# The up products of a gated MLP: copied out of PSUM by ScalarE and multiplied in SBUF, instead of multiplied out of PSUM by VectorE

## The chip, the core and the metric

The kernel runs on one core of a Trainium2 chip. The metric is the device time of one execution in microseconds (us), as the median of several runs. Engines are named as in the profile: PE (TensorE; PEld is its weight load), ACT (ScalarE), DVE (VectorE), POOL (GpSimd), SP (SyncE, which issues the DMAs here).

## What is computed

```python
xn = _layernorm(x)                                   # x: 2048 x 512, bfloat16
return x + _A_ref(xn, wqkv, w_phi, wo) + _B_ref(xn, w_gate, w_up, w_down)

# A: linear attention, 32 heads of 16
pq = einsum("bhsd,hdf->bhsf", q, w_phi); pk = einsum("bhsd,hdf->bhsf", k, w_phi)
phi_q = concat([softmax(pq), softmax(-pq)]);  phi_k = concat([softmax(pk), softmax(-pk)])
kv = einsum("bhsf,bhsd->bhfd", phi_k, v);  z = sum of phi_k over s
o = (phi_q @ kv) / (phi_q @ z + 1e-6);  A = o @ wo

# B: gated MLP, hidden width 1792
g = xn @ w_gate;  u = xn @ w_up;  B = (g * u) @ w_down
```

The change touches `g * u` alone.

## The kernel before, in words

Tokens come in 16 tiles of 128 (index t) and in 4 groups of 512 (index g). All inputs are loaded once by DMAs that SP issues at the start; everything then lives in SBUF. PSUM has 8 banks of 128 x 512 fp32.

- `emit_ln_stats` and `emit_xn` (lines 403 to 433): DVE takes mean and variance (L406, L408, L412), POOL the power -0.5 (L414), DVE normalises (L428), PE transposes the tile by four 128x128 matmuls, ACT copies the result out of PSUM into `xnT`.
- `k_pe` (L494): the V product of a tile, 4 matmuls of 128x512, copied out by ACT.
- `k_pk` and `q_pk` (L499, L575): the K and Q products with the feature map folded into the weights (`wprime`, L438), 4 matmuls each. Then `emit_exp` (L451): ACT copies the product twice, plain and negated, into SBUF; DVE takes a maximum tree (L464, four steps) and subtracts it (L470); ACT takes the exponential of 128x1024.
- `k_norm`, `q_scale` (L504, L580): sums (L484), reciprocals and scalings on DVE.
- `emit_kv` (L540): the K-V products, 8 matmuls of 128x65 per head group and half.
- `q_T`, `q_num`, `q_oT` (L592 to L611): a DMA transposes the weights of a tile, PE takes 8 small matmuls of 128x68, DVE divides (L602, L603), another DMA transposes the result into `oT`.
- `glu` (L520): 56 pieces, 4 token groups by 14 blocks of 128 hidden units. A piece is two products of 4 matmuls of 128x512, gate into bank `bg` and up into bank `bu`. ACT copies the gate bank to a bfloat16 tile `gr` in a ring of three (L531); DVE multiplies the up bank by `gr` into `hT` (L533). The pieces turn through banks 5, 6 and 7; those of the last token group through 5 and 6.
- `final` (L616): the output of a tile, 14 matmuls over `hT` and 4 over `oT` into one bank; DVE adds x (L635), and a DMA stores the tile.

ACT operations all carry the line of the helper `act_op`, L273; all matmuls have L292; DMAs have L162 (transposes) and L163.

What sets the order: all these steps are recorded first. `_order` (L696) then lists them engine by engine, with a planned cost for each: it takes whatever step can start first, and among those of an engine that are equally early the one of least priority number. Copies out of a product bank of `glu` and the multiplication have priority -1, ahead of everything else that is ready. The matmuls of `glu` have priorities of 1e6 and more and those of `final` of 2e6 and more, so PE takes them when nothing else is ready. The order that results is fixed in the program: each engine runs its list strictly in turn, and `_emit_all` (L752) puts semaphore waits where a step depends on another engine. A changed cost or a changed dependence thus changes the lists of every engine.

Of the kernel before, what the change touches and what calls it, by code (L numbers as in the profile page):

```python
# [8 lines left out]
ALU = mybir.AluOpType  # L9
# [184 lines left out]
def _build(nc, es, A_x, A_wqkv, A_w_phi, A_wo, B_w_gate, B_w_up, B_w_down, out):  # L194
# [59 lines left out]
    def sbv(name, lo, n):  # L254
        off = layout[name] + lo
        return arena[:, off:off + n]
# [5 lines left out]
    def bank(b, lo=0, n=512):  # L262
        return psum[:, b * 512 + lo: b * 512 + lo + n]
# [4 lines left out]
    def act_op(out_ap, in_ap, func=ACTF.Copy, scale=1.0, bias=None, prio=None):  # L268
        def fn(e):
            kw = {}  # L270
            if bias is not None:
                kw["bias"] = bias
            return e.activation(out=out_ap, in_=in_ap, func=func, scale=scale, **kw)  # L273
        r = [in_ap]
        if isinstance(scale, bass.AP):
            r.append(scale)
        if isinstance(bias, bass.AP):
            r.append(bias)
        return sc.step(ACT, fn, reads=r, writes=[out_ap], cost=50.0 + 0.833 * in_ap.free_size(), lat=180.0, prio=prio)

    def dve(fn, reads, writes, n, rate=1.0, fixed=65.0, prio=None):
        return sc.step(DVE, fn, reads=reads, writes=writes, cost=fixed + rate * n / 0.96, lat=150.0, prio=prio)
# [4 lines left out]
    def mms(items, prio=None, warm=False):  # L287

        def fn(e):
            ins = None  # L290
            for o, l, r, a, z in items:
                ins = e.matmul(o, lhsT=l, rhs=r, start=a, stop=z)  # L292
            return ins
        reads = []
        writes = []
        c = 0.0
        for o, l, r, a, z in items:
            reads += [l, r]
            writes.append(o)
            c += max(25.0, o.free_size() / 2.4 + 2.3) * (1.6 if warm else 1.0)  # L300
        return sc.step(PE, fn, reads=reads, writes=writes, cost=c, lat=260.0, prio=prio)

    def group(o, pairs):
        n = len(pairs)
        return [(o, l, r, i == 0, i == n - 1) for i, (l, r) in enumerate(pairs)]
# [13 lines left out]
    def xnT(q, s_lo, n):  # L319
        return sbv("xnT", q * S_TOK + s_lo, n)  # L320
# [62 lines left out]
    for jt in range(NQ):  # L383
        pool(lambda e, jt=jt: e.tensor_tensor(
            out=wbd_v[:, jt, :].rearrange("p (g f b) -> p g f b", g=2, b=4),
            in0=wphi_v[:, jt, None, :, None].to_broadcast([128, 2, 16, 4]),
            in1=bind8.rearrange("p (g b) -> p g b", g=2)[:, :, None, :].to_broadcast([128, 2, 16, 4]), op=ALU.mult),
# [127 lines left out]
    def hT(g, ft, lo, n):  # L515
        return sbv("hTa" if g < 2 else "hTb", ((g % 2) * NF + ft) * 512 + lo, n)
# [3 lines left out]
    def glu(g, ft, banks):  # L520
        i = glu_ctr[0]
        glu_ctr[0] += 1
        bg = banks[(2 * i) % len(banks)]
        bu = banks[(2 * i + 1) % len(banks)]
        gr = sbv("gring", (i % 3) * 512, 512)
        base = 1e6 + i * 10
        mms(group(bank(bg), [(wg_v[:, q, ft * 128:(ft + 1) * 128], xnT(q, g * 512, 512)) for q in range(NQ)]),
            prio=base)
        mms(group(bank(bu), [(wu_v[:, q, ft * 128:(ft + 1) * 128], xnT(q, g * 512, 512)) for q in range(NQ)]),
            prio=base + 1)  # L530
        act_op(gr, bank(bg), prio=-1.0)  # L531
        dst = hT(g, ft, 0, 512)
        dve(lambda e: e.tensor_tensor(out=dst, in0=bank(bu), in1=gr, op=ALU.mult), [bank(bu), gr], [dst], 512,  # L533
            prio=-1.0)


# [106 lines left out]
    def some_glu(n, g_max):  # L643
        for _ in range(n):
            if units and units[0][0] <= g_max:
                glu(*units.pop(0), (5, 6, 7) if units and units[0][0] < 3 else (5, 6))
# [189 lines left out]
```

## Time and profile before

| | |
|---|---|
| median of 3 runs | 229.64 us (229.61 to 229.78) |
| profiled execution | 230.12 us, of which the span of the profile is 228.0 us |
| clock granted to PE | 1.00 in every slice |
| ACT 128x512 out of PSUM | 160 of 608 ns (L273) |
| ACT 128x1024 exponential | 32 of 1061 ns (L273) |
| DVE 128x512 product out of PSUM | 56 of 681 ns (L533) |
| DVE waiting for ACT at L464 | 2.0 us in all |
| ACT waiting for DVE at L470 | 28.1 us in all, 14 times |
| ACT waiting for PE | 45.7 us in all, 48 times |

The engines' busy times are unions of the rows' durations. Two instructions that follow each other on ACT or DVE overlap in these rows: six copies of 128x512 that ACT makes one after another take 3.04 us, so one starts about 0.48 us after the other although each row lasts 0.6 us. The same holds for DVE (a row of 0.68 us, the next one 0.60 us later).

### The profile page before, as it was taken

The numbers are of one execution on the slowest core, as the hardware profiler recorded it, in microseconds if no ns is written. First come the engines' busy times: TensorE is split into PE (matmuls) and PEld (weight loads), VectorE is DVE, ScalarE is ACT, GpSimd is POOL, SyncE is SP. The second block draws the span as 40 slices with busy tenths as digits, with TensorE's granted clock in tenths as the row PEclk, the third lists the DMA queues.
The fourth block names the chain that finished last, engine by engine and source line by source line (L and its number), as shares of the span: only waits on it lengthen the run. The fifth ranks groups of instructions, "written<-read, shape, count | busy, mean of one in ns | idle before, by whom it ended". The sixth has DMA issues, their size and how long they took to land.

```text
span 228.0 us, 3617 instructions
## 1 busy us (share of the span) xinstructions
PE 219.0 (96%) x1306; PEld 108.9 (48%) x1330; DVE 193.7 (85%) x554; ACT 119.7 (52%) x201; POOL 8.2 (4%) x22
## 2 busy tenths in 40 slices
PE   8899799999999999999999999999999999998994
PEld 8454354444454555444464444444445444444441
DVE  4548999999997999999986999999999999993321
ACT  2587997735449987944528585464653331110000
POOL 5301000000011000000000000000000000000000
PEclk9999999999999999999999999999999999999999
DMA  6999970000000000000000035554144545468301
GB/s 181 249 285 369 379 249 1 0 0 0 0 3 1 0 3 0 0 3 0 0 4 0 0 65 96 85 94 103 36 92 105 118 92 116 92 126 110 88 23 46
DMA packets 39697, 18.33 MB, mean 80 GB/s; under 512 B 30720, under 2 KB 38656, under 8 KB 39680
## 3 DMA queue, kind: packets, MB, share of 16 engines
q1 hardware_dynamic: 39152, 18.09, 32.5%
q8 instruction: 10, 0.16, 0.3%
q10 hardware_dynamic: 528, 0.02, 0.1%
q14 instruction: 7, 0.06, 0.1%
HBM read 8.67 MB, written 2.10 MB: 47 GB/s over the span
## 4 chain that ended last, share of the span: by engine, by line
PE 85%; SPq 6%; DMA 5%; DVE 1%; issue 1%; ACT 1%
PE ps L292 85%; SPq L162 4%; DMA arena<-in_A_x_dram 3%; DMA arena<-arena 2%; SPq L163 1%; ACT arena L273 1%; DVE arena L464 1%; DVE arena L406 0%; DVE arena L635 0%; DVE arena L470 0%
## 5 line engine op out<-in xcount | busy, mean ns | idle before, releaser
L292 PE MATMUL ps<-arena 128*128 128x512 bf16 (+3 forms) x1306 | 219.0, 328 | 6.1 <-ACT arena L273 2.4
L292 PEld LDWEIGHTS ps<-arena 128*128 128x128 bf16 x1330 | 108.9, 100 | 115.7 <-DVE arena L533 2.3
L273 ACT ACTIVATE arena<-ps 128x512 bf16<-128x512 f32 (+1 forms) x168 | 88.0, 590 | 50.6 <-PE ps L292 45.7
L484 DVE TENSOR_TENSOR arena<-arena 128x512 f32<-128x512 bf16 (+3 forms) x128 | 49.3, 395 | 0.2
L273 ACT ACTIVATE arena<-arena 128x1024 bf16<-128x1024 bf16 x32 | 34.0, 1061 | 29.0 <-DVE arena L470 28.1
L533 DVE TENSOR_TENSOR arena<-ps,arena 128x512 bf16<-128x512 f32 x56 | 38.1, 681 | 2.2 <-PE ps L292 1.6
L464 DVE TENSOR_TENSOR arena<-arena 128x128 bf16<-128x128 bf16 (+3 forms) x128 | 31.7, 269 | 2.2 <-ACT arena L273 2.0
L470 DVE TENSOR_TENSOR arena<-arena 128x1024 bf16<-128x1024 bf16 x32 | 21.6, 676 | 0.0
L635 DVE TENSOR_TENSOR arena<-ps,arena 128x512 bf16<-128x512 f32 x16 | 11.0, 688 | 11.8 <-PE ps L292 11.5
L406 DVE BATCH_NORM_STATS2 arena<-arena 128x6 f32<-128x512 bf16 x16 | 10.5, 682 | 6.8 <-DMA arena<-in_A_x_dram 6.8
L603 DVE TENSOR_TENSOR arena<-ps,arena 128x512 bf16<-128x512 f32 x16 | 10.9, 680 | 0.1
L511 DVE TENSOR_TENSOR arena<-arena 128x1024 bf16<-128x1024 bf16 x16 | 10.9, 680 | 0.0
L602 DVE RECIPROCAL arena<-ps 128x32 f32<-128x32 f32 x16 | 5.6, 350 | 4.6 <-PE ps L292 4.3
L508 DVE RECIPROCAL arena<-arena 128x64 bf16<-128x64 f32 x16 | 8.7, 543 | 0.1
L428 DVE TENSOR_SCALAR arena<-arena 128x512 bf16<-128x512 bf16 x16 | 5.9, 409 | 2.2 <-POOL arena L414 2.0
L414 POOL TENSOR_TENSOR arena<-arena 128x1 f32<-128x1 f32 (+1 forms) x7 | 5.2, 750 | 60.7 <-DVE arena L412 60.7
L589 DVE TENSOR_TENSOR arena<-arena 128x512 bf16<-128x512 bf16 x16 | 6.6, 414 | 0.0
L586 DVE RECIPROCAL arena<-arena 128x32 f32<-128x32 f32 x16 | 5.5, 342 | 0.0
L587 DVE TENSOR_TENSOR arena<-arena 128x32 bf16<-128x32 f32 x16 | 2.7, 171 | 0.0
L273 ACT ACT_TABLE_LOAD x1 | 1.3, 1283 | 1.3 <-PEq L821 1.3
L408 DVE BATCH_NORM_AGGREGATE arena<-arena 128x2 f32<-128x6 f32 x16 | 1.9, 162 | 0.0
L551 DVE TENSOR_TENSOR arena<-arena 128x64 bf16<-128x64 f32 x8 | 1.7, 214 | 0.0
(18 smaller groups left out, 8.4 us busy)
## 6 DMA issues: line engine op xcount, KB each, us to landing
out_dram<-arena SPq DMA_DIRECT2D x16, 128.0 KB, 1.7
arena<-in_B_w_down_dram SPq DMA_DIRECT2D x1, 1792.0 KB, 15.4
arena<-in_B_w_gate_dram SPq DMA_DIRECT2D x1, 1280.0 KB, 9.1
arena<-in_B_w_up_dram SPq DMA_DIRECT2D x1, 1280.0 KB, 11.9
arena<-in_A_x_dram SPq DMA_DIRECT2D x1, 1024.0 KB, 6.5
arena<-in_A_x_dram SPq DMA_DIRECT2D x2, 256.0 KB, 3.2
arena<-in_A_wqkv_dram SPq DMA_DIRECT2D x1, 512.0 KB, 5.2
arena<-in_B_w_gate_dram SPq DMA_DIRECT2D x1, 512.0 KB, 4.4
```

What stands on the lines that cost most here:

```text
L162: return e.dma_start_transpose(out_ap, in_ap)
L273: return e.activation(out=out_ap, in_=in_ap, func=func, scale=scale, **kw)
L292: ins = e.matmul(o, lhsT=l, rhs=r, start=a, stop=z)
L406: dve(lambda e, t=t: e.bn_stats(stats_v[:, t, 0:6], x_tile(t)), [x_tile(t)], [stats_v[:, t, 0:6]], 512)
L464: dve(lambda e, dst=dst, src=src, k=k: e.tensor_tensor(out=dst, in0=src[:, :, 0:k], in1=src[:, :, k:2 * k], op=ALU.max), [src], [dst], 16 ...
L470: dve(lambda e: e.tensor_tensor(out=p4, in0=p4, in1=src[:, :, None, :].to_broadcast([128, 16, 16, 4]), op=ALU.subtract), [pst, src], [pst] ...
L484: dve(lambda e, dst=dst, src=src, k=k: e.tensor_tensor(out=dst, in0=src[:, :, 0:k], in1=src[:, :, k:2 * k], op=ALU.add), [src[:, :, 0:2 * ...
L508: dve(lambda e: e.reciprocal(out=rs, in_=sm), [sm], [rs], 64, rate=8.0)
L511: dve(lambda e: e.tensor_tensor(out=e4, in0=e4, in1=r4[:, :, None, :].to_broadcast([128, 16, 16, 4]), op=ALU.mult), [ek_v[:, t, :], rs], [ ...
L533: dve(lambda e: e.tensor_tensor(out=dst, in0=bank(bu), in1=gr, op=ALU.mult), [bank(bu), gr], [dst], 512, prio=-1.0)
L603: dve(lambda e: e.tensor_tensor(out=o.rearrange("p (g h d) -> p g h d", g=8, h=4), in0=nd[:, :, 0:64].rearrange("p g (h d) -> p g h d", h= ...
L635: dve(lambda e: e.tensor_tensor(out=og, in0=bank(b), in1=x_tile(t), op=ALU.add), [bank(b), x_tile(t)], [og], 512, prio=-2.0)
```

## The change

```diff
         act_op(gr, bank(bg), prio=-1.0)
         dst = hT(g, ft, 0, 512)
-        dve(lambda e: e.tensor_tensor(out=dst, in0=bank(bu), in1=gr, op=ALU.mult), [bank(bu), gr], [dst], 512,
+        act_op(dst, bank(bu), prio=-1.0)
+        dve(lambda e: e.tensor_tensor(out=dst, in0=dst, in1=gr, op=ALU.mult), [dst, gr], [dst], 512, rate=0.5,
             prio=-1.0)
```

Each of the 56 pieces gets a second ACT copy, which puts the up product as bfloat16 where the result will stand. DVE then multiplies that tile in place by the gate tile, both bfloat16 in SBUF. The planned cost of the multiplication is halved (`rate=0.5`). An up bank is free again when ACT has copied it, no longer when DVE has multiplied it. Since the costs and the dependences differ, `_order` also makes another order; how many instructions each engine runs is otherwise the same.

## The prediction

> **What bounds the kernel now.** The page's busy times name PE:
>
> ```profile
> PE 219.0 (96%) x1306; PEld 108.9 (48%) x1330; DVE 193.7 (85%) x554; ACT 119.7 (52%) x201; POOL 8.2 (4%) x22
> ```
>
> PE's waits, from the view of who waited for whom (total us, times, longest), come to under 5 us:
>
> ```profile
> PE ps L292 <- ACT arena L273: 2.4, 3, 1.6
> PE ps L292 <- DVE arena L363: 1.1, 1, 1.1
> PE ps L292 <- DMA arena<-arena: 0.8, 1, 0.8
> PE ps L292 <- DVE arena L428: 0.5, 2, 0.3
> ```
>
> And two pieces of the chain that ended last (start, length, what, matmuls):
>
> ```profile
> 118.20 10.74 PE ps L292 x49
> ...
> 217.81 7.30 PE ps L292 x33
> ```
>
> A busy PE need not be a full PE, since matmul rows overlap (379 ns each). The chain settles it: 49 recorded matmuls of 128x512 in 10.74 us are one per 219 ns, and start to start the trace shows 216 ns with one record lost in each such piece. So PE runs at its own rate from 24.89 us to its end at 225.1 us (217.81 + 7.30), but for one gap of 0.81 us before 208.01. The other waits lie before 24.9 us, the largest being 1.64 us. The change takes no matmul away, so **the floor does not move**: it can win at most the two gaps, 1.64 + 0.81 = 2.45 us, and it can lose as much as ACT holds PE up.
>
> **The two gaps.** The timeline of the first (start, length, engine, instruction, idle before):
>
> ```profile
> 22.49 0.68 DVE L470 TENSOR_TENSOR arena<-arena 128x1024 bf16<-128x1024 bf16 x1
> ...
> 23.20 1.06 ACT L273 ACTIVATE arena<-arena 128x1024 bf16<-128x1024 bf16 x1 [2.10 <-DVE arena L470]
> 23.87 0.68 DVE L533 TENSOR_TENSOR arena<-ps,arena 128x512 bf16<-128x512 f32 x1
> 24.17 1.06 ACT L273 ACTIVATE arena<-ps 128x512 bf16<-128x512 f32 x2
> 24.47 0.68 DVE L470 TENSOR_TENSOR arena<-arena 128x1024 bf16<-128x1024 bf16 x1
> ...
> 24.89 0.60 PE L292 MATMUL ps<-arena 128*128 128x128 bf16 x5 [1.64 <-ACT arena L273]
> ```
>
> PE stops at 23.09 (its last matmul starts at 22.875) because the transposition of token tile 7 needs a bank that ACT empties at 24.17, and in ACT's list that copy stands behind the exponential of 23.20, which needed DVE's subtraction of 22.49. The second gap:
>
> ```profile
> 207.44 1.24 SPq L162 DMA_TRANSPOSE arena<-arena  x1
> ...
> 208.01 1.29 PE L292 MATMUL ps<-arena 128*128 128x68 bf16 x11 [0.81 <-DMA arena<-arena]
> ```
>
> A transposed weight tile (t = 14) landed at 207.97 while PE had nothing ahead of it in its list but that. Its first parts had landed at 206.08; a 16 KB packet of the queue q8, which fetches instructions, ran from 205.62 for 1.39 us on one of the DMA engines.
>
> **The change part by part.** Durations are those of the groups kept apart by shape:
>
> ```profile
> L273 ACT ACTIVATE arena<-ps 128x512 bf16<-128x512 f32 x160 | 86.9, 608 | 50.6 <-PE ps L292 45.7 <-DVE arena L484 4.3
> L533 DVE TENSOR_TENSOR arena<-ps,arena 128x512 bf16<-128x512 f32 x56 | 38.1, 681 | 2.2 <-PE ps L292 1.6 <-ACT arena L273 0.2
> L273 ACT ACTIVATE arena<-arena 128x1024 bf16<-128x1024 bf16 x32 | 34.0, 1061 | 29.0 <-DVE arena L470 28.1 <-DMA arena<-arena 0.9
> ...
> L464 DVE TENSOR_TENSOR arena<-arena 128x512 bf16<-128x512 bf16 x32 | 13.3, 416 | 2.0 <-ACT arena L273 2.0
> ```
>
> *VectorE.* 56 rows of 681 ns become 56 of the bfloat16 form in SBUF, whose nearest row is the first step of the maximum tree, 416 ns at the same shape: 38.1 - 56 x 0.416 = 38.1 - 23.3 = 14.8 us less work, 193.7 to about 179 us. None of it is on PE's path where PE is full: worth 0 there.
>
> *ScalarE.* 56 more copies of 608 ns: 34.0 us, 119.7 to about 154 us (67%). At the spacing of 0.48 us that copies in a row show (six in 3.04 us) it is 27 us. One piece asks PE for 8 x 0.216 = 1.73 us and ACT for 0.96 instead of 0.48 us. In the K stage a tile costs PE 4 + 4 matmuls and a transposition, 1.95 us, and ACT four copies and an exponential at 0.96 us, 2.9 us; the 28 pieces of the first two token groups, spread over the last 12 tiles (2.33 a tile), make this PE 5.98 against ACT 5.14 us, 86%, where it was 4.0 us, 67%. So on the average of every stage **ACT stays under PE**, with a thin margin in the K stage. Taking the order into account, two stretches of 6 us are full already (columns: PE, PEld, DVE, ACT, POOL):
>
> ```profile
> 30.00:36.00 6.00, 5.95 (x35) 2.94 (x34) 6.00 (x15) 6.00 (x12) 0.00 (x0) 1.00 0.48 150
> ...
> 72.00:78.00 6.00, 5.95 (x34) 2.99 (x34) 5.74 (x18) 5.96 (x11) 0.00 (x0) 1.00 0.00 0
> ```
>
> *The first gap, by the new lists.* Up to the second matmul group of piece 1 PE's list is unchanged, so PE is free at 23.09 as before. Then it has piece 2 and piece 3 (16 matmuls, not 4) ahead of the transposition of tile 7. Up 2 and gate 3 find their banks emptied (copies at about 20.5 and 21.4) and fill 2 x 0.864 us, to 24.82. Up 3 needs gate 2's copy. ACT's list has it behind the exponentials of tiles 0 and 1. The first still starts at 23.20. The second's subtraction no longer stands behind a multiplication of 0.60 us on DVE: it ends at 24.55 instead of 25.15; exponential 24.58 to 25.54, copy to 26.15. PE loses 26.2 - 24.82 = 1.38 instead of 1.80 us (24.89 - 23.09): 0.42 better. But ACT then has nine copies and an exponential queued, and the next tiles' products need the copies of tiles 6 and 7, which it reaches at 30.3 and 31.3: 0.17 and 0.07 late, and about 0.05 for one bank before: 0.3 worse. I take **-0.1 us**. Bounds: -1.64 (no gap left) and +0.96 (one exponential more ahead of a needed copy). No load is late: piece 4, which moves up from 35.6 to about 28.2 us, needs weights that landed at 23.8 and 27.2; 1 us of cover.
>
> *The second gap.* DVE and ACT get through the Q stage earlier against PE: after the last group of 128x68 PE has 137 matmuls left instead of 65, 29.6 us. The last transposed tiles are then no longer needed at once. **-0.8 us**; bounds -0.81 and 0. SP's list keeps its order of transposes and stores and issues nothing more. But the q8 fetches come about every 20 us whatever the order (ten in the trace, at 143.1 and 163.1 among them), and a transposed tile in flight then lands up to 1.4 us late; the tiles of t = 5 and 9 come close to those two, with 0.6 us and more of room: **+0.1 us** (0 to 0.8). [...]
>
> *New waits in the middle.* Both banks of a piece now wait for one engine. Where ACT stands at an exponential whose subtraction is not done (14 times, 28.1 us, in the row ACT <- DVE L470), two copies a piece stand behind it instead of one, and DVE can no longer empty the up bank. With banks 5 to 7 PE runs one and a half pieces, 2.6 us, ahead. Most of those waits are harmless because the list puts an exponential only where ACT had nothing else. I take **+0.3 us**; bounds 0 and +1.9 (four copies of 0.48 us in the two full stretches, all pushed on to PE).
>
> *Sum.* -0.1 - 0.8 + 0.1 + 0.3 = -0.5 us: 230.12 to 229.6 us in the profiled execution. The median, 0.48 us under that execution, goes to **229.1 us**. What lies after PE's last matmul (0.69 us of DVE and the last store) is unchanged.
>
> **Rivals.**
> 1. *The gap only moves.* Another transposed tile is hit, or the second gap is partly the profiled execution's own (it is the slower one by 0.48 us); the rest as above. 229.64 - 0.1 + 0.3 = 229.8, between 229.3 and 230.0. For it: q8's fetches stay. Against it: 14 of the 16 tiles were in time before.
> 2. *ACT becomes the bound in the K stage* (other side). The place is the stretches 30 to 36 and 72 to 78 us, where ACT has no idle time; it decides once ACT is asked for more than PE's time over a stretch longer than the 2.6 us that the banks cover. Four copies more there cost 1.9 us; with the second gap gone: 229.64 + 1.9 - 0.8 = 230.7, 231.5 with it. For it: 86% on average leaves little for uneven work. Against it: PE's list was made anew with the new costs. [...]
> 3. *Both gaps close*: 229.64 - 1.64 - 0.81 + 0.3 = 227.5. It needs exponential 0 earlier than 23.20, and what precedes it (x landing at 20.55, DVE's queue) is untouched.
>
> That the multiplication keeps its 681 ns is possible, but then PE is full all the same and the time is that of rival 1.
>
> **How the numbers follow.** A measurement of this kernel can tell about 0.2% (0.46 us) from no change, so faster means under 229.18. Forecast (228.6 to 229.5): 0.48, of it 0.31 faster and 0.17 same. Rival 1: 0.22, same but for 0.03 faster. Rival 2: 0.22, slower but for 0.02 same. Rival 3: 0.08, faster. Together faster 0.42, same 0.38, slower 0.20. The range takes in the forecast, rival 1 and the lower half of each of the others: 228.2 to 230.7.
>
> **What would show it.** L534 near 416 ns; ACT 154 us; PE <- ACT still with a wait near 25 us, of 1.4 instead of 1.6 us; no PE <- DMA after 200 us. Wrong: PE <- ACT or PEld <- ACT with many waits between 30 and 130 us (rival 2), PE <- DMA earlier (rival 1), a first wait well under 1 us (rival 3).

## The result, and the profile after

The changed kernel takes **230.37 us** (median, 230.24 to 230.68), the kernel before in the same rounds 229.63 us: ratio 1.0033, 95% interval 1.0022 to 1.0043. It is 0.74 us slower. The forecast was 229.1 us (228.2 to 230.7). The profiled execution took 230.26 us with a span of 228.3 us (before 230.12 and 228.0), PE at a granted clock of 1.00. In some executions of four of the kernels below the granted clock was 0.992 or 0.993 instead of 0.998 to 1.000, and these took 231.6 to 232.9 us; without them the median of the kernel with the change in the Q stage alone is 230.14 instead of 230.29 us, and that of the kernel with x loaded earlier 230.28 instead of 231.01 us.

Busy times of the engines:

```profile
PE 218.8 (96%) x1306; PEld 107.1 (47%) x1330; DVE 180.9 (79%) x554; ACT 145.7 (64%) x257; POOL 8.4 (4%) x22
```

Groups, forms kept apart (busy us, mean ns | idle before, and whom it waited for):

```profile
L273 ACT ACTIVATE arena<-ps 128x512 bf16<-128x512 f32 x216 | 116.3, 633 | 29.2 <-PE ps L292 27.9 <-DVE arena L484 0.4
L273 ACT ACTIVATE arena<-arena 128x1024 bf16<-128x1024 bf16 x32 | 34.9, 1089 | 9.3 <-DVE arena L470 9.2
L534 DVE TENSOR_TENSOR arena<-arena 128x512 bf16<-128x512 bf16 x56 | 23.5, 420 | 2.7 <-ACT arena L273 2.6
```

The operations cost what the prediction said: the multiplication 420 ns, 12.8 us less on DVE, 26.0 us more on ACT, which is 56 times 0.46 us. ACT's wait for subtractions fell from 28.1 to 9.2 us: it no longer stands idle, it has work. Whom PE waits for (total us, times, longest):

```profile
PE ps L292 <- ACT arena L273: 2.0, 4, 1.0
PE ps L292 <- DVE arena L428: 1.3, 1, 1.3
PE ps L292 <- DVE arena L363: 1.1, 1, 1.1
PE ps L292 <- DMA arena<-arena: 1.0, 1, 1.0
```

PE's own timeline from 20 us on (start, length, instruction, matmuls; in brackets the idle time before, where the rows show one):

```profile
25.82 47.24 PE L292 MATMUL ps<-arena 128*128 128x512 bf16 x247 [1.00 <-ACT arena L273]
73.31 66.29 PE L292 MATMUL ps<-arena 128*128 128x512 bf16 x438 [0.24 <-ACT arena L273]
140.60 84.82 PE L292 MATMUL ps<-arena 128*128 128x68 bf16 x465 [1.00 <-DMA arena<-arena]
```

The reader is to see three things. The gap near 25 us is there, smaller. The gap of 208 us is gone, and one of 1.00 us stands before 140.60 instead. And there is a break at 73.31 where before had none. A row of a matmul lasts longer than its turn (379 against 216 ns), so waits under about 0.15 us hide in these lines. Taken start to start (216 ns for a 128x512; records missing from the trace taken out), between 36 and 110 us PE stands 0.67 us: 0.10 at 46.24, 0.05 at 71.17, 0.19 at 73.09, 0.15 at 89.21, all for a bank that ACT has yet to empty (the first matmul after the third wait is missing from the trace, so its row begins at 73.31), and 0.18 at 107.74 for DVE's copy of the K-V products. Before, the same count finds nothing between 36 and 207 us.

The start, with the gap that the prediction worked out:

```profile
22.62 1.06 ACT L273 ACTIVATE arena<-arena 128x1024 bf16<-128x1024 bf16 x1 [0.84 <-DVE arena L470]
...
24.00 1.06 ACT L273 ACTIVATE arena<-arena 128x1024 bf16<-128x1024 bf16 x1 [0.32 <-DVE arena L470]
...
24.96 2.04 ACT L273 ACTIVATE arena<-ps 128x512 bf16<-128x512 f32 x4
...
25.82 6.42 PE L292 MATMUL ps<-arena 128*128 128x512 bf16 x30 [1.00 <-ACT arena L273]
```

Two exponentials, then the copy of gate 2, and PE goes on: the order that was foretold. All of it lies earlier than foretold because the second half of x (tiles 8 to 15), whose statistics stand in DVE's list ahead of the first subtraction, landed at 19.97 us, in the execution of before at 20.55. That is 0.58 us of chance between the two profiles, and so they differ by only 0.3 us in their spans while the medians differ by 0.74.

The new gap, in the chain that ended last, and SP beside it:

```profile
135.78 4.78 DMA arena<-arena
140.55 0.05 issue
140.60 5.18 PE ps L292 x30
```

The transposed tile t = 4 took 4.78 us from its issue to its landing (the median of the 32 transposes of this trace is 3.0 us). Its parts landed from 138.79 to 140.55; a 16 KB packet of q8, a fetch of instructions, ran from 138.34 for 1.28 us. (The page gives the kind `instruction` to q8, with 10 packets and 0.16 MB, and to q14, with 7 and 0.06 MB.) In before the fetch of 205.62 stood so beside t = 14.

What ACT does to PE, by stretches (PE, PEld, DVE, ACT and POOL busy us, clock, DMA share, GB/s), first before, then after:

```profile
36.00:48.00 12.00, 11.95 (x56) 5.42 (x56) 11.95 (x30) 8.19 (x15) 0.00 (x0) 1.00 0.00 0
...
sum 72.00, PE 71.63 PEld 34.66 DVE 69.49 ACT 48.53 POOL 2.02; mean PE 11.94 PEld 5.78 DVE 11.58 ACT 8.09 POOL 0.34
```

```profile
36.00:48.00 12.00, 11.95 (x56) 5.32 (x56) 11.71 (x41) 11.76 (x22) 0.00 (x0) 1.00 0.00 0
...
sum 72.00, PE 71.37 PEld 34.88 DVE 66.92 ACT 63.40 POOL 2.13; mean PE 11.89 PEld 5.81 DVE 11.15 ACT 10.57 POOL 0.35
```

Between 36 and 108 us ACT went from 48.5 to 63.4 of 72 us, 88%. It is not the bound on the average, but it is nearly full, and its list is strictly in turn. At one of the breaks:

```profile
71.38 1.16 ACT L273 ACTIVATE arena<-arena 128x1024 bf16<-128x1024 bf16 x1
...
72.32 2.66 ACT L273 ACTIVATE arena<-ps 128x512 bf16<-128x512 f32 x5
...
73.08 1.41 PEld L292 LDWEIGHTS ps<-arena 128*128 128x128 bf16 x8 [0.51 <-ACT arena L273]
...
73.31 1.46 PE L292 MATMUL ps<-arena 128*128 128x512 bf16 x6 [0.24 <-ACT arena L273]
```

The second copy of the row of five empties the bank; it stands behind an exponential and another copy, with no idle time on ACT in between.

### The profile page after: what moved, and what is told of

Read it like the earlier page. It is cut to its first block, busy times and chain, and to the rows that moved or that the text cites. A ratio compares the mean times of both kernels' runs of the same rounds, so it can differ in the third digit from the quotient of the medians.

```text
span 228.3 us, 3639 instructions
## 1 busy us (share of the span) xinstructions
PE 218.8 (96%) x1306; PEld 107.1 (47%) x1330; DVE 180.9 (79%) x554; ACT 145.7 (64%) x257; POOL 8.4 (4%) x22
## 4 chain that ended last, share of the span: by engine, by line
PE 81%; SPq 6%; DMA 5%; DVE 4%; ACT 3%; issue 1%
PE ps L292 81%; SPq L162 4%; ACT arena L273 3%; DMA arena<-in_A_x_dram 3%; DMA arena<-arena 2%; SPq L163 1%; DVE arena L464 1%; DVE arena L470 1%; DVE arena L484 0%; DVE arena L406 0%; DVE arena L636 0%; DVE arena L604 0%; DVE arena L603 0%; DVE arena L534 0%; DVE arena L587 0%
## 5 line engine op out<-in xcount | busy, mean ns | idle before, releaser
L292 PEld LDWEIGHTS ps<-arena 128*128 128x128 bf16 x1330 | 107.1, 99 | 117.9 <-ACT arena L273 7.2
L273 ACT ACTIVATE arena<-ps 128x512 bf16<-128x512 f32 (+1 forms) x224 | 117.2, 619 | 29.2 <-PE ps L292 27.9
L484 DVE TENSOR_TENSOR arena<-arena 128x128 f32<-128x128 f32 (+3 forms) x128 | 49.4, 396 | 1.1 <-ACT arena L273 0.8
L273 ACT ACTIVATE arena<-arena 128x1024 bf16<-128x1024 bf16 x32 | 34.9, 1089 | 9.3 <-DVE arena L470 9.2
L464 DVE TENSOR_TENSOR arena<-arena 128x256 bf16<-128x256 bf16 (+3 forms) x128 | 31.2, 272 | 2.0 <-ACT arena L273 1.8
L636 DVE TENSOR_TENSOR arena<-ps,arena 128x512 bf16<-128x512 f32 x16 | 11.1, 691 | 26.0 <-PE ps L292 25.8
L534 DVE TENSOR_TENSOR arena<-arena 128x512 bf16<-128x512 bf16 x56 | 23.5, 420 | 2.7 <-ACT arena L273 2.6
L604 DVE TENSOR_TENSOR arena<-ps,arena 128x512 bf16<-128x512 f32 x16 | 10.9, 679 | 0.1
L428 DVE TENSOR_SCALAR arena<-arena 128x512 bf16<-128x512 bf16 x16 | 6.0, 409 | 2.6 <-POOL arena L414 2.3
L590 DVE TENSOR_TENSOR arena<-arena 128x512 bf16<-128x512 bf16 x16 | 6.5, 403 | 0.0
```

What stands on the lines that cost most here:

```text
L464: dve(lambda e, dst=dst, src=src, k=k: e.tensor_tensor(out=dst, in0=src[:, :, 0:k], in1=src[:, :, k:2 * k], op=ALU.max), [src], [dst], 16 ...
L484: dve(lambda e, dst=dst, src=src, k=k: e.tensor_tensor(out=dst, in0=src[:, :, 0:k], in1=src[:, :, k:2 * k], op=ALU.add), [src[:, :, 0:2 * ...
L534: dve(lambda e: e.tensor_tensor(out=dst, in0=dst, in1=gr, op=ALU.mult), [dst, gr], [dst], 512, rate=0.5, prio=-1.0)
L604: dve(lambda e: e.tensor_tensor(out=o.rearrange("p (g h d) -> p g h d", g=8, h=4), in0=nd[:, :, 0:64].rearrange("p g (h d) -> p g h d", h= ...
L636: dve(lambda e: e.tensor_tensor(out=og, in0=bank(b), in1=x_tile(t), op=ALU.add), [bank(b), x_tile(t)], [og], 512, prio=-2.0)
```

## The experiments

Theory A: a fetch of instructions that falls on a transposed tile makes that tile late, and which tile it falls on follows from how many instructions PE has issued, not from the clock. Theory F: the gap near 25 us is there because DVE's list stands at the statistics of tiles whose load has not landed. Theory G: the waits between 36 and 110 us come from ACT's work a tile, since ACT alone now empties the banks of a piece. Other theories are told in the expectations. "Before" is each time the kernel before, timed beside the run.

### The fetches moved, by the warm-up alone

The 50 matmuls that warm PE up at the start become fewer and longer, or more and shorter, with the same columns in all. Only the number of PE's instructions ahead of the work changes.

```diff
-    warm = sbv("tree", 0, 128)
-    mms([(bank(7, 0, 128), warm, warm, True, True)] * 50, warm=True)
+    warm = sbv("tree", 0, 256)
+    mms([(bank(7, 0, 160), warm[:, 0:128], warm[:, 0:160], True, True)] * 40, warm=True)   # changed form
+    mms([(bank(7, 0, 104), warm[:, 0:128], warm[:, 0:104], True, True)] * 62, warm=True)   # before form
```

> The changed kernel, but PE's 50 warm-up matmuls of 128x128 at the start are 40 of 128x160: 20 PE rows fewer for the same columns, so each instruction fetch on q8 should come about 1.6 us later against PE's work, and the lists of all engines are otherwise the same. Theory A (the 1.16 us gap at 139 us is a fetch that delays one transposed tile, t = 4): the fetch comes at about 140 us, after that tile has landed, the gap goes, no wait of PE for a DMA over 0.3 us is left, 230.37 - 1.0 = 229.4 us. Rival B (the gap comes from SP's queue or from the tile being late anyway): the gap stays, 230.4 us.

> The kernel before, but with 62 warm-up matmuls of 128x104 instead of 50 of 128x128: 24 PE rows more, so each fetch should come about 1.9 us earlier against PE's work; the lists are otherwise the same. Theory A (the 0.81 us gap before 208 us is the fetch at 205.6 us hitting the tile t = 14): it goes, 229.63 - 0.8 = 228.8 us, unless another tile is hit. Rival B: it stays, 229.6 us.

Measured: the changed form 229.44 us, ratio to before 0.9976 (0.9965 to 0.9986); the before form 228.76 us, 0.9956 (0.9930 to 0.9982). PE in the changed form:

```profile
26.24 47.47 PE L292 MATMUL ps<-arena 128*128 128x512 bf16 x247 [0.76 <-ACT arena L273]
73.95 150.93 PE L292 MATMUL ps<-arena 128*128 128x512 bf16 x903 [0.24 <-ACT arena L273]
```

and in the before form:

```profile
28.09 198.09 PE L292 MATMUL ps<-arena 128*128 128x512 bf16 x1147 [0.22 <-issue]
```

No line waits for a transposed tile any more, in either. The fetch that stood at 138.3 us came at 140.7, after tile 4 had landed at 139.63; that of 205.6 (now 205.4) began 0.34 us before its tile was issued, and the tile took 3.21 us. The medians agree with the gaps: against its own before the changed form gains 1.0033 - 0.9976 = 0.57%, 1.3 us, where a gap of 1.16 us went; the before form gains 0.44%, 1.0 us, where one of 0.97 us went. **Theory A holds.** With neither form hit, the changed one is 0.68 us slower by the medians, about what the breaks between 36 and 110 us add up to (0.67 us in the profile after, 0.66 us here). The times alone don't show it: by the ratios it is 0.0020 or 0.46 us, and the before form's interval is 0.6 us to either side. (The before form's profile is of an execution of 231.68 us; of it the times of tile and fetch and the absence of gaps are used.)

The traces of all 14 kernels say more. Instructions are also fetched on a second queue, q14, in packets of 8 KB; the page of after has (packets, MB, share of the DMA engines' time):

```profile
q8 instruction: 10, 0.16, 0.3%
q14 instruction: 7, 0.06, 0.1%
```

Of 448 transposes after 60 us, 335 had no fetch of either queue between issue and landing, and none of these took more than 3.42 us. All that took longer had one, up to 4.89 us. PE waited 15 times for a transposed tile in these traces, 14 times for one with a fetch in flight; the other wait is of 0.20 us. Not every fetch does harm: of 73 tiles with one of q8 in flight 44 took over 3.6 us, the others mostly being issued after the fetch had begun or landing just as it began.

### The new form in one stage alone

```diff
+        if g < 2:        # the other kernel: g >= 2
             act_op(dst, bank(bu), prio=-1.0)
             dve(lambda e: e.tensor_tensor(out=dst, in0=dst, in1=gr, op=ALU.mult), [dst, gr], [dst], 512, rate=0.5,
                 prio=-1.0)
+        else:
+            dve(lambda e: e.tensor_tensor(out=dst, in0=bank(bu), in1=gr, op=ALU.mult), [bank(bu), gr], [dst], 512,
+                prio=-1.0)
```

> The change for the 28 pieces of token groups 0 and 1 alone (those that run beside the K stage); the other 28 multiply out of PSUM as before. Theory A (ACT holds PE up in the K stage, where it has 86% of PE's time to do): PE waits for ACT between 36 and 110 us add up to about 0.5 us as in the changed kernel (0.7); 230.1 us, give or take 0.8 us for where the DMA gap falls. Rival C (the loss comes from the Q stage): no such waits over 0.1 us in all, about 229.6 us.

> The change for the 28 pieces of token groups 2 and 3 alone. Theory A: PE does not wait between 36 and 104 us (under 0.1 us in all), and the time is that of before but for where the DMA gap falls: 229.6 us, 228.8 us without a gap, 230 us with a larger one. Rival C: 230.3 us or more, with PE waiting for ACT after 104 us.

Measured: token groups 0 and 1 (those of the K stage) in the new form 229.64 us, 0.9979 (0.9964 to 0.9995); groups 2 and 3 in the new form 230.29 us, 1.003 (1.0005 to 1.0055). The first has the breaks of the full change (0.10 at 47.4, 0.19 at 74.2, 0.15 at 90.4, 0.17 at 110.6) and no wait for a tile. The second has none between 36 and 110 us and 0.17 at 114.6; its time is in tiles that came late, 0.33 + 0.82 + 0.13 us at t = 6, 7 and 11, beside fetches at 153.3 (q14), 161.7 and 181.9. So, by the gaps, the lasting cost is the K stage's, and the Q stage's half moves the time by which tiles are hit. The medians can't show it: the kernel that has the K stage's breaks is the faster one, because no tile of it was late.

### A planner that knows the exponential, and a fourth bank

The planned cost of the exponential is raised by 58 ns to what the rows show (0.96 us to the start of the next row in before); and, in another kernel, pieces of the first two groups turn through four banks, the other products through four instead of five.

```diff
-        return sc.step(ACT, fn, reads=r, writes=[out_ap], cost=50.0 + 0.833 * in_ap.free_size(), lat=180.0, prio=prio)
+        return sc.step(ACT, fn, reads=r, writes=[out_ap], cost=(108.0 if func == ACTF.Exp else 50.0) + 0.833 * in_ap.free_size(), lat=180.0, prio=prio)
```

```diff
-        b = a_bank[0] % 5
+        b = a_bank[0] % 4
-                glu(*units.pop(0), (5, 6, 7) if units and units[0][0] < 3 else (5, 6))
+                glu(*units.pop(0), (4, 5, 6, 7) if units and units[0][0] < 2 else (5, 6, 7) if units and units[0][0] < 3 else (5, 6))
```

> The changed kernel with one planned cost altered: an exponential of 128x1024 counts as 961 ns, as ACT's rows are spaced (0.96 us), not as 903; nothing but the order differs. Theory D (the 0.67 us that PE waits for ACT between 36 and 110 us come from a plan that is too short by 0.06 us at each exponential): those waits fall under 0.2 us. Theory E (they come from ACT having too much to do beside banks 5 to 7, whatever the plan knows): 0.4 to 0.9 us stay. The time is 230.4 less what goes, give or take 1 us for where the fetches fall.

> The changed kernel with PSUM banks shared out otherwise in the K stage: the pieces of token groups 0 and 1 turn through banks 4 to 7 instead of 5 to 7, and the tile products through 0 to 3 instead of 0 to 4. Theory E (ACT holds PE up because three banks cover only one and a half pieces): PE's waits for ACT between 36 and 110 us fall from 0.67 to under 0.2 us. If the load on ACT alone decides, they stay above 0.5 us. The start, where the tile products have one bank less, may lose about 0.5 us.

Measured: 230.55 us, 1.0040 (1.0024 to 1.0056), and 231.75 us, 1.0086 (1.0067 to 1.0105). With the better cost the waits for ACT between 36 and 110 us fall from 0.49 to 0.34 us, between what theories D and E gave, and the order is another one: how much of them is the planner's misjudgement stays open. Tiles t = 5 and 12 were late (0.20 and 1.18 us, the first with no fetch in flight, the second beside one at 181.2). The fourth bank decided nothing: between 36 and 110 us 0.28 us of waits for ACT stay, 0.31 us for DVE come and 0.20 us before 39.45 that the trace puts down to neither, the start waits 0.98 us for the load of up weights that landed at 27.15 us (a piece now comes before its weights), and two tiles were hit (0.75 and 0.93 us). Four banks move pieces ahead of what they need, which is another change than more room.

### The V copies off ScalarE

```diff
-        act_op(vext_all[:, t, :, 0:64], bank(b).rearrange("p (c j) -> p c j", c=8))
+        vd = vext_all[:, t, :, 0:64]
+        vs = bank(b).rearrange("p (c j) -> p c j", c=8)
+        dve(lambda e: e.tensor_copy(out=vd, in_=vs), [vs], [vd], 512)
```

> The changed kernel with the 16 copies of the V products out of PSUM on DVE instead of ACT: 16 x 0.48 = 7.7 us less on ACT in the K stage, 16 x 0.60 = 9.6 us more on DVE. Theory G (the amount of ACT's work in the K stage makes PE wait): waits of PE for ACT between 36 and 110 us fall from 0.67 to under 0.2 us; the time is 230.4 - 0.6 = 229.8 us, give or take 1 us for where the fetches fall. Rival H (DVE is as full there, so PE waits for DVE instead): waits of PE for DVE of 0.5 us and more appear there.

Measured: 230.89 us, 1.0045 (1.0016 to 1.0075). Taking one copy a tile from ACT leaves one wait for ACT between 36 and 110 us, 0.18 us at 105.84. Between 36 and 108 us PE has 71.98 of the 72 us:

```profile
sum 72.00, PE 71.98 PEld 35.07 DVE 65.37 ACT 60.49 POOL 2.50; mean PE 12.00 PEld 5.84 DVE 10.89 ACT 10.08 POOL 0.42
```

The waits went as theory G has it. But the order changed with the edit, and the K stage lasts longer: the sixteenth exponential, the last of the K stage, starts at 116.0 us instead of 99.4 in the changed form. So ACT's work fell by the copies and by a slower pace of the tiles, and the run does not part the two. The time got no better, since DVE, with the V copies, came later to the first tiles (a gap of 2.62 us before 23.07) and another tile was late (1.47 us before 146.4).

### The start: the load of x, and VectorE's list

The before form with its fetches moved, x loaded one place earlier in SP's list:

```diff
-    load_wT(0)
     load_x(8, 8)
+    load_wT(0)
```

> The kernel before with the 62 warm-up matmuls of 128x104 of an earlier run here, and the load of x tiles 8 to 15 issued ahead of the transposing load of the Q weights. Theory F (the first gap, 1.6 to 2.5 us before 25 us, ends a given time after the load of x tiles 8 to 15 has landed, since DVE's list stands at their statistics): the load lands at about 17 instead of 20.5 us and the gap falls under 0.8 us; 227.7 us against 228.8 with the warm-up alone, if no fetch hits a transposed tile. Rival: the gap has another cause and stays, 228.8 us.

Measured: 231.01 us, 1.0053 (1.0027 to 1.0078). The forecast failed. The load landed at 18.60 us, earlier than the 20.55 of before but not at 17, and the gap grew: PE waits 3.3 us for DVE's normalisation (L428), until 21.87.

```profile
18.62 0.69 DVE L406 BATCH_NORM_STATS2 arena<-arena 128x6 f32<-128x512 bf16 x1 [1.50 <-DMA arena<-in_A_x_dram]
...
21.87 2.35 PE L292 MATMUL ps<-arena 128*128 128x128 bf16 x16 [3.28 <-DVE arena L428]
```

DVE's list does stand at the statistics until the load lands, as theory F has it, but in the order that came out the normalisation that PE needs stands behind them as well. The kernels that share their list at the start show the tie better. The wait near 25 us ends 4.34 us after the landing in before and with its fetches moved, and 4.33 in the Q stage's kernel (landings at 20.55, 21.59 and 20.42 us); it ends 5.85 us after it in the changed form and in the K stage's kernel, and 5.63 in the changed form with its fetches moved (19.97, 21.12 and 20.61). The next pair leaves the loads alone and tells the planner that this one lands 3.5 us later, so that the statistics stand further down in DVE's list (before form on the 62 matmuls, changed form on the 40):

```diff
+            if st.nbytes == 8 * 131072:
+                st.finish += 3500.0
```

> The before form with the warm-up of the run before_fetch_moved (228.76 us, no PE gap after 36 us), and the planner told that the second half of the x load lands 3.5 us later than it thinks, so that it no longer puts the statistics of token tiles 8 to 15 in VectorE's list ahead of the first subtractions; every wait stays. Theory F (the gap near 25 us exists because VectorE's in-order list stands at statistics of tiles whose load lands at 20.0 to 21.6 us, and the first exponential and the copies behind it stand behind that): the time that PE loses between 8 and 36 us goes from 2.5 to 3 us to about 1.5 to 2, and the time to about 227.8 us, 0.8% under the kernel before; 1 us more if a fetch of instructions falls on a transposed weight tile again. Rival H (PE would wait there anyway, for the bank that ScalarE empties or for the transposition of the tiles): the loss between 8 and 36 us stays at 2.5 us or more, 228.8 us.

> The changed form with the warm-up of the run after_fetch_moved (229.44 us, no PE <- DMA gap) and the same planner setting. Theory F: the loss between 8 and 36 us shrinks by about 1 us here too, to 228.5 us; the waits for ScalarE in the K stage (0.4 to 0.5 us) stay, so it ends about 0.7 us behind the before form of the same call. Rival (the waits in the K stage only make up for what the start lost, so a kernel with a better start has more of them): no nearer than 1.2 us to the before form. Rival H: no gain, 229.4 us.

Measured: the before form 229.88 us, 0.9999 (0.9980 to 1.0017); the changed form **228.37 us, 0.9937 (0.9919 to 0.9956)**, faster than both kernels. Waits of PE, before form, then changed form:

```profile
PE ps L292 <- DVE arena L363: 1.1, 1, 1.1
PE ps L292 <- ACT arena L273: 1.1, 3, 0.6
PE ps L292 <- DMA arena<-arena: 1.0, 2, 0.8
PE ps L292 <- DVE arena L428: 1.0, 2, 0.8
```

```profile
PE ps L292 <- DVE arena L363: 1.1, 1, 1.1
PE ps L292 <- ACT arena L273: 0.9, 3, 0.4
PE ps L292 <- DVE arena L428: 0.3, 1, 0.3
```

PE's loss between 8 and 36 us is 2.14 and 1.10 us, where before has 2.93 and the changed form 2.27 to 2.96: theory F holds for the start, with less won in the before form than forecast (1.5 to 2). The before form got nothing of it, because the new order put two tiles beside fetches (waits of 0.39 and 0.98 us at 143.0 and 184.3, fetches at 139.9 and 182.2). The changed form was to end 0.7 us behind; it ended 1.5 us ahead, 1.37 us of it these two tiles. Its waits for ACT between 36 and 110 us are 1.0 us, twice what they were: the longest is 0.56 us before 43.23. So a part of what the start wins is given back there, as the rival had it.

### Once more the fetches, and once more the V copies

The before form of the last pair with 74 matmuls of 128x88 to warm up; the changed form of the last pair with the V copies on DVE.

> The before form of the run before_no_x_wait, whose fetches came at 139.9 and 182.2 us and held two transposed tiles (PE waits of 0.40 and 0.98 us after 140 us), with a warm-up of 74 matmuls of 128x88 instead of 62 of 128x104, so that the fetches come about 3 us earlier (near 137, 158, 179 and 200 us). Theory A (which tile a fetch holds decides what a form of the kernel takes here): no PE <- DMA wait over 0.2 us after 140 us, 228.5 us (229.88 - 1.38). Rival (the tiles are late because VectorE feeds them late in this order): the two waits stay, 229.9 us. Beside the changed form in this setting (228.37 us in the call before) it tells whether the two forms then differ: by the added gaps (start and middle 2.21 us here, 2.17 us there) they do not, within 0.3 us.

> The changed form of the run after_no_x_wait (228.37 us; PE waits for ScalarE between 36 and 110 us: 0.18, 0.56, 0.11, 0.15 = 1.0 us), with the copies of the V products moved from ScalarE to VectorE. Theory G (in the K stage these waits exist because ScalarE's in-order list holds the product banks, and its work a tile decides): the waits between 36 and 110 us fall to 0.2 us or less, about 0.8 us gained, 227.6 us, unless a fetch again holds a transposed tile (then 1 us more). Rival (they come from the order in which the planner puts the pieces): they stay near 1 us, 228.4 us.

Measured: the before form 228.97 us, 0.9964 (0.9949 to 0.9978); the changed form 228.58 us, 0.9941 (0.9926 to 0.9957). In the before form the two late tiles are in time again and 0.9 us of time is won, but two others wait, 0.33 us (t = 1, a fetch at 137.3 beside it) and 0.41 us (t = 4, landed at 157.76; the nearest fetch of q8, at 158.8, comes after it, but one of 8 KB on q14 ran from 156.21 for 0.82 us). So theory A holds here only with both queues counted. The expectation of this run gives the before form 2.21 us of gaps at the start and in the middle; that leaves out a wait of 0.21 us for ACT before 30.41, so it is 2.42 us, against 2.15 for the changed form. In the changed form the waits for ACT between 36 and 110 us go from 1.0 to 0.14 us, as theory G has it a second time (and again with a slower pace, the sixteenth exponential at 111.0 instead of 102.4 us):

```profile
PE ps L292 <- DVE arena L363: 1.1, 1, 1.1
PE ps L292 <- DVE arena L499: 0.8, 3, 0.3
PE ps L292 <- DVE arena L428: 0.6, 2, 0.4
PE ps L292 <- ACT arena L273: 0.2, 1, 0.2
```

It gains no time, because the start loses 2.10 instead of 1.10 us, 1.25 of it, start to start, in the three waits for the V copies on DVE (L499): the work was moved from one full list to another.

### The account

Gaps of PE in the profiled execution against the profile of before (2.93 us of loss between 8 and 36 us, x landed at 20.55 us, no gap from 36 to 132 us, 0.97 us start to start for the late tile). The start is put to an equal landing of x, one us for one us: the same list lost 2.27 us where x landed at 19.97 and 2.96 where it landed at 20.61. All in us.

| kernel | start | 36 to 132 | late tiles | sum | medians |
|---|---|---|---|---|---|
| after | -0.08 | +0.67 | +0.19 | +0.78 | +0.74 |
| after, fetches moved | -0.03 | +0.66 | -0.97 | -0.34 | -0.54 |
| K stage alone | -0.04 | +0.66 | -0.97 | -0.35 | -0.34 |
| Q stage alone | -0.06 | +0.17 | +0.31 | +0.42 | +0.31 |
| planner knows the exponential | -0.07 | +0.45 | +0.41 | +0.79 | +0.72 |
| four banks | +0.34 | +0.79 | +0.71 | +1.84 | +1.92 |
| before, no x wait | -0.95 | +0.28 | +0.44 | -0.23 | -0.11 |
| after, no x wait | -1.40 | +1.05 | -0.97 | -1.32 | -1.62 |
| before, no x wait, fetches moved | -0.88 | +0.27 | -0.23 | -0.84 | -0.87 |
| after, no x wait, V copies on DVE | -0.60 | +0.31 | -0.97 | -1.26 | -1.26 |

Three kinds of gap account for every time here to 0.3 us and for most to 0.12. Each row sets one profiled execution beside a median over several, so differences of 0.2 us between rows say little. Three kernels are left out, since their profiled executions took 2.9 and 1.2 us more and 0.8 us less than their medians: the before form with its fetches moved, the V copies on DVE with the old start, and x loaded earlier.

## Why the prediction was wrong, point by point

The forecast was 229.1 us and the measured time 230.37. Of these 1.27 us, 0.89 lie in the fetches (the second gap and the other tiles) and 0.37 in the middle. That 230.37 lies inside 228.2 to 230.7 is owed to the room that the range leaves for the rivals, not to the forecast.

- **The floor does not move**: right. PE runs at 216 ns a matmul in both kernels, and all that differs is gaps.
- **VectorE and ScalarE**: right as costs. L534 took 420 ns (416 forecast), DVE 180.9 us (179). ACT 145.7 us: the prediction gave 154 by the rows and 27 us more by the spacing of copies; the spacing was the right one (26.0).
- **The first gap, -0.1**: right. Piece 3's up product waits for the copy of gate 2 behind two exponentials, and k_pe of tiles 6 and 7 wait 0.21 and 0.11 us (forecast 0.17 and 0.07). At an equal landing of x it comes to -0.08.
- **The second gap, -0.8, and +0.1 for other tiles**: this is the step that failed. That the tiles after 200 us would have room was right: there is no wait there. But I took the fetches at before's times ("about every 20 us whatever the order", 143.1 and 163.1), and looked only for tiles near those. They came with PE's instructions: the seventh at about the 1719th row of PE and PEld in before and the 1706th after, the tenth at the 2464th and the 2435th, and so at 143.1 and 138.3, 205.6 and 200.4 us, as PE's list puts other work there. At 138.3 stood tile 4: 1.16 us instead of the forecast 0.1, beyond its bound of 0.8. Together +0.19 instead of -0.7. The trace of before alone told against a fixed time: its ten fetches lie 17.2 to 29.4 us apart, and 196 to 274 of these rows; in the trace after it is 16.3 to 25.8 us and 209 to 273 rows. PE itself shows no stop at a fetch: eight of before's ten began between 36 and 207 us, where its rows have no gap. But a transposed tile beside one cost PE 0.97 us start to start in before and 1.16 us after.
- **New waits in the middle, +0.3**: the mechanism was right, the term too small: 0.67 us. Of it 0.49 are the full ACT list, near the stretch of 72 to 78 us that was pointed out and two others; 0.18 is a wait for DVE at the head of the Q stage that the prediction did not have. With the V copies moved off ACT the waits for ACT fell to 0.18 and 0.14 us. "Most of those waits are harmless because the list puts an exponential only where ACT had nothing else" was half of it: ACT now nearly always has something else (it waits 9.2 us for subtractions where it waited 28.1).
- **Rivals**: it is rival 1 (the gap moves) with the middle of rival 2 at a third of its size, 229.64 - 0.08 + 0.67 + 0.19 = 230.4. The prediction has the two together only at rival 2's full size (231.5 us); at a third of it they had no case. Where no fetch hits, the two forms are on rival 2's side: the changed one is 0.68 us slower by the medians and 0.66 us by the middle's gaps. The pair without the x wait is not: 0.9937 (0.9919 to 0.9956) for the changed form against 0.9964 (0.9949 to 0.9978) for the before form with its fetches moved, each against its own before, while by the account's gaps other than late tiles it is -0.35 for the changed form against -0.61 and, with the earlier warm-up, -0.67 us for the before form. There the sign of the times is not settled.

**What stays open**: why a tile beside a fetch takes as long as it does (1.76 us between its first and last part for a fetch of 1.28 us), and whether the 0.49 us of waits for ACT come from its work a tile alone or also from the order and the pace at which the planner put the tiles.

## What to carry to other kernels

Where the bound engine is full, list its gaps start to start and ask of each what sets its moment: here the fetches went with PE's rows (the seventh at about the 1719th and the 1706th, 143.1 and 138.3 us), and new orders put them beside other transfers, worth about 1 us either way (0.97 us won, 1.16 us lost) and not to be credited to the change. Here ACT went from 67% to 88% of the stretch that matters, and its in-order list, which alone gives back the banks of a piece, cost PE 0.49 us there; price such an engine by that stretch and by what stands in its list, not by the average. Before a time is explained by a change, run both forms with the accident removed: here that showed -1.0 us for before, -1.3 us for after, and about 0.7 us for the change itself, the last resting on the gaps more than on the times.

## What the runs showed of the hardware that was not expected

- Fetches of 16 KB on q8 (ten in a run) held up DMA transposes in flight. In the profiles of the two kernels a fetch took 0.93 to 1.39 us. The 47 transposes between SBUF tiles that had no fetch in flight, of 64, took at most 3.25 us; the seven during which one of 16 KB began took 3.51 to 4.89 us. The longest, 4.89 us (t = 14, before) and 4.78 us (t = 4, after), had it begin 2.55 and 2.56 us after their issue. Beside fetches of 8 KB on q14 stood waits of 0.33 us (change in the Q stage alone) and 0.41 us (before, no x wait, fetches moved). Ten matmuls fewer at the start of the changed kernel, with the same columns in all, moved the fetch beside t = 4 from 138.3 to 140.7 us and the time by 0.57% (ratios 0.9976, 0.9965 to 0.9986, and 1.0033, 1.0022 to 1.0043).
- The load of the second half of x landed between 19.97 us (after) and 21.59 us (before, fetches moved) in the six profiles named above that issue the loads in the same order; about as much is lost at the start (the same list lost 2.27 us with a landing at 19.97 and 2.96 us at 20.61). So two single profiles are compared only after their loads are.
